# Attention and squared-ReLU FFN in one program: where values are staged, when one square and one pair of transposes run, and which banks hold the last rows

## The chip, the cores and the metric

One core of a Trainium2 chip runs the whole program. The metric is the device time of one execution in microseconds (us); the figure for a kernel is the median of its runs. TensorE (PE) multiplies, ScalarE (ACT) and VectorE (DVE) empty PSUM and do the elementwise work, GpSimd (POOL) casts what has been loaded, and two queues issue transfers: SyncE's (SP) and, for some loads, ScalarE's.

## What is computed

```python
# q, k, v: (8 batches, 8 heads, 576 rows, 64), float32
scores = scale * q @ k.T
mask = (rel >= 0) & (rel < 64)            # causal, window of 64
attn = softmax(where(mask, scores, -1e9))
x = (attn @ v) as (4608 rows, 512)        # heads side by side
h = maximum(x @ w_in, 0)                  # (4608, 2048)
out = (h * h) @ w_out                     # (4608, 512), float32
```

## The kernel before

The 4608 rows are 36 chunks of 128; four chunks make a block of 512 rows, so there are nine blocks, 0 to 8. Two chunks make a pair; pairs 8 and 15 (chunks 16, 17 and 30, 31) are tails, each chunk of which gathers the last 64 rows of two sequences.

**One chunk.** Its k, q and v rows are loaded as float32 into staging tiles (`fetch_kq` L138, `fetch_v` L144, `fetch_tail` L148), cast to fp16 on POOL (`cast_k`, `cast_q`, `cast_v`, through `copy` L248 to L254), turned by DMA transposes on SP (`dma_kT` L345, `dma_qT` L356), multiplied to scores (`S_`, L376), exponentiated on ACT (`expo`, L382), masked on DVE (`keep`, L387), multiplied by v (`V`, L399) and divided by the row sums on DVE (`norm`, L406 and L407). The result x_sb is turned into a part of xT. From block 4 on that is a DMA transpose (`dma_xT`, L426). In the blocks up to 3 it is four TensorE transposes into a PSUM tile (`X`, L418) and a copy out of it on DVE (`copy_xT`).

**One block of the FFN.** The up product has 16 steps (`UP` L474): four matmuls of 512 columns into one of two PSUM buffers (tag `ps_u`, L477), then ReLU on ACT (hrelu, L481), then the square: on ACT for even steps (L483), on DVE for odd ones (L485). DVE reads the PSUM buffer again, so an odd step's buffer is free only after its square. The down product of a block (`out_seven` L534) uses seven half-size products of 8 steps instead of eight. They run in the order A, A again, B, C, D, C again, D again, each product in two halves of 8 matmuls of 256 columns (L556). The first product of A is copied from PSUM to SBUF as p1 by ACT (p, L570), and the second product then goes on adding into the same bank. The other sums u2, u4 and the output rows are made on DVE (L572). The last block uses another bank, E, for the second product, and issues its last product one row half m after the other (`rows_apart` L606, matmuls L608).

**PSUM and staging.** `ps_u`, `ps_o` and `ps_att` have two buffers each; a `ps_att` tile (`att_bank`) is two banks. The staging tag `st` has five single tiles: v of a chunk, q of a tail, and the sums p1, u2 and u4 of the FFN take turns in it. The tag `st2` has six double tiles: k and q of a chunk, or k k and v v of a tail chunk. A tile that is allocated again waits for the readers of what was in it.

**Order.** It is fixed in the program: every engine has a queue in program order. The start (blocks 0 and 1 of the up product, block 0's output) is the hand-written list FIRST. After it, the loop over g from 2 to 9 merges by place in the stage (0 to 1): the 14 steps of `out_seven(g-1)`, the 16 steps UP(g, f), `attention(g+1)` and `loads`. `later(n, fn)` L87 puts an instruction n ticks back; a tick comes after each UP, each half product and each attention step. A stage thus begins with the scores of two chunks, the two halves of A's first product with UP(g, 0) and UP(g, 1) between and behind them, then the copy p.

```python
ev += [(t + 0.02, lambda a=a: sc(a)), ...
       (t + 0.25, lambda a=a: va(a)), (t + 0.251, lambda b=b: va(b)),
       (t + 0.275, lambda a=a: to_xT(a)), (t + 0.276, lambda b=b: to_xT(b))]
```

Here t is 0 or 0.46 for a block's two pairs, and 0.1 more for block 3. v of chunks 22 and up is issued from ACT's queue, everything else from SP's.

Of the kernel before, what the change touches and what calls it, by code (L numbers as in the profile page):

```python
# [41 lines left out]
def kernel(  # L42
# [9 lines left out]
    nc = tc.nc  # L52
# [32 lines left out]
    put_off = []  # L85

    def later(n, fn):  # L87
        put_off.append([n, fn])

    def tick():  # L90
        for e in list(put_off):
# [30 lines left out]
    def fetch_pair(nm, p):  # L122
# [9 lines left out]
        for n in range(2):  # L132
            sts[nm, 2 * p + n] = st[:, :, n, :]

    def two_tiles():
        return stage.tile([P, 2, H, D], FP32, name="kq_st", tag="st2", bufs=6)

# [4 lines left out]
            fetch_rows(sts[nm, i], src, *place(i), eng=eng)  # L142

    def fetch_v(i, eng=nc.sync):  # L144
        sts["v", i] = stage.tile([P, H, D], FP32, name="v_st", tag="st", bufs=5)
        fetch_rows(sts["v", i], v, *place(i), eng=eng)

    def fetch_tail(i):  # L148

        kk, vv = two_tiles(), two_tiles()  # L150
        qv = stage.tile([P, H, D], FP32, name="q_st", tag="st", bufs=5)
        sts["k", i], sts["q", i], sts["v", i] = (kk[:, 0], kk[:, 1]), qv, (vv[:, 0], vv[:, 1])
        b = tail_seq(i)
        for n in range(2):
            fetch_rows(kk[:, n], k, b + n, S - 128)
        for n in range(2):
            fetch_rows(qv[:], q, b + n, S - 64, 64, 64 * n)
        for n in range(2):
            fetch_rows(vv[:, n], v, b + n, S - 128, eng=nc.scalar if i >= 22 else nc.sync)

# [99 lines left out]
        copy(eng, q16s[i][:], sts["q", i])  # L262

    def cast_v(i, eng=nc.gpsimd):
        copy(eng, v_evs[i % NV][:, :, 0:D], sts["v", i][:])

    def shift_v(i, eng=nc.gpsimd):
        v_ev, v_od, v_next = v_evs[i % NV], v_ods[i % NV], v_ods[(i + 1) % NV]
# [205 lines left out]
    def UP(g, f):  # L474
        hps = ps_up.tile([P, 512], FP32, name="hps", tag="ps_u")
        for c in range(DMC):
            nc.tensor.matmul(  # L477
                hps[:], w_in_sb[:, c, f * P:(f + 1) * P], xT_of(g)[:, c, :],
                start=(c == 0), stop=(c == DMC - 1))
        hrelu = hrp.tile([P, 512], FP32, name="hrelu", tag="hrelu")  # L480
        nc.scalar.activation(out=hrelu[:], in_=hps[:], func=AF.Relu)  # L481
        if f in SQ_ACT:
            nc.scalar.activation(out=h2_of(g)[:, f, :], in_=hrelu[:], func=AF.Square)  # L483
        else:
            nc.vector.scalar_tensor_tensor(  # L485
                out=h2_of(g)[:, f, :], in0=hps[:], scalar=0.0, in1=hrelu[:],
                op0=ALU.max, op1=ALU.mult)
        tick()
# [45 lines left out]
    def out_seven(g):  # L534
        h2 = h2s[g]
        TH = 256
        top = (slice(0, TH), slice(0, KH)), (slice(0, TH), slice(KH, FFC))
        bot = (slice(TH, 512), slice(0, KH)), (slice(TH, 512), slice(KH, FFC))
        A = [[h2[:, ks, ts] for ts, ks in row] for row in (top, bot)]
        Sh = [hs_all[:, i] for i in range(2)]  # L540
        Sh += [A[1][0], A[0][1]]
        banks, sums, osb = {}, {}, {}

        def hsum(i, half):
            ks = slice(half * KH // 2, (half + 1) * KH // 2)
            x, y, op = ((A[1][0], A[1][1], ALU.add), (Sh[0], A[0][0], ALU.subtract),
                        (A[0][0], A[1][0], ALU.subtract), (A[0][1], Sh[1], ALU.subtract))[i]
            nc.vector.tensor_tensor(out=Sh[i][:, ks], in0=x[:, ks], in1=y[:, ks], op=op)  # L548

        def product(bank, a, w, half, first):  # L550
            if first and half == 0:
                pool, tag = (ps_up, "ps_u") if bank == "E" else (ps_out, "ps_o")
                banks[bank] = pool.tile([P, 2, NH], FP32, name=f"ops{bank}", tag=tag)
            for kk in range(half * KH // 2, (half + 1) * KH // 2):
                for m in range(2):
                    nc.tensor.matmul(  # L556
                        banks[bank][:, m, :], a[:, kk, m * P:(m + 1) * P], w[:, kk],
                        start=(first and kk == 0 and m == 0), stop=(kk == KH - 1),
                        skip_group_check=True)

        def evac(bank, to, add=None, row=0, col=0, send=False, ms=slice(0, 2)):
            if to == "osb":
                if row not in osb:
                    osb[row] = next_osb()
                dst = osb[row][:, ms, col * NH:(col + 1) * NH]
            else:
                sums[to] = stage.tile([P, 2, NH], FP32, name=to, tag="st", bufs=5)
                dst = sums[to][:]
            if add is None:
                nc.scalar.activation(out=dst, in_=banks[bank][:], func=AF.Copy, scale=OUT_SCALE)  # L570
            else:
                nc.vector.scalar_tensor_tensor(  # L572
                    out=dst, in0=banks[bank][:, ms], scalar=OUT_SCALE, in1=sums[add][:, ms],
                    op0=ALU.mult, op1=ALU.add)
            if send:
                cols = slice(col * NH, (col + 1) * NH) if last else slice(0, DM)
                if is_tail(4 * g + 2 * row):
                    ov = out.rearrange("(b s) d -> b s d", s=S)
                    for n in range(2):
                        b0 = tail_seq(4 * g + 2 * row) + n  # L580
                        nc.sync.dma_start(
                            out=ov[b0:b0 + 3:2, S - 64:S, cols].rearrange("m s d -> s m d"),
                            in_=osb[row][64 * n:64 * n + 64, :, cols])
                else:
                    b, s0 = place(4 * g + 2 * row)
                    r0 = b * S + s0
                    nc.sync.dma_start(
                        out=out[r0:r0 + TH, cols].rearrange("(m p) d -> p m d", p=P)[:, ms],
                        in_=osb[row][:, ms, cols])

        W = [[w_out_sb[:, 0:KH, 0:NH], w_out_sb[:, 0:KH, NH:DM]],
             [w_out_sb[:, KH:FFC, 0:NH], w_out_sb[:, KH:FFC, NH:DM]]]
        last = g == NTB - 1
        plan = [
            ("A", A[0][0], W[0][0], True, (("A", "p1"),)),
            (("E", A[0][1], W[1][0], True, (("E", "osb", "p1", 0, 0, last),)) if last else
             ("A", A[0][1], W[1][0], False, (("A", "osb", None, 0, 0),))),
            ("B", Sh[1], wb[0], True, (("B", "u2", "p1"),)),
            ("C", Sh[0], W[0][1], True, (("C", "u4", "u2"),)),
            ("D", Sh[2], wb[1], True, (("D", "osb", "u4", 1, 1, last),)),  # L600
            ("C", Sh[3], W[1][1], False, (("C", "osb", "u2", 0, 1, True),)),
            ("D", A[1][1], wb[2], False, (("D", "osb", "u2", 1, 0, True),)),
        ]
        before = {0: (0, 1), 2: (2,), 3: (3,)}
        steps = []
        def rows_apart(bank, a, w, m, evs):  # L606
            for kk in range(KH):
                nc.tensor.matmul(banks[bank][:, m, :], a[:, kk, m * P:(m + 1) * P], w[:, kk],  # L608
                                 start=False, stop=(kk == KH - 1), skip_group_check=True)
            for e in evs:  # L610
                evac(*e, ms=slice(m, m + 1))

        for n, (bank, a, w, first, evs) in enumerate(plan):
            if last and n == len(plan) - 1:
                steps += [lambda m=m, args=(bank, a, w): rows_apart(*args, m, evs) for m in range(2)]
                break
            for half in range(2):
                def step(n=n, bank=bank, a=a, w=w, first=first, evs=evs, half=half):
                    for i in before.get(n, ()):
                        hsum(i, half)  # L620
                    product(bank, a, w, half, first)
                    if half == 1:
                        for e in evs:
                            evac(*e)
                    tick()
                steps.append(step)
        return steps
# [24 lines left out]
    def attention(g):  # L652
        c = 4 * g
        ev = []

        def sc(i):
            S_(i)
# [17 lines left out]
        for h in range(2):  # L675
            a, b, t = c + 2 * h, c + 2 * h + 1, 0.46 * h + (0.1 if g == 3 else 0.0)
            ev += [(t + 0.02, lambda a=a: sc(a)), (t + 0.021, lambda b=b: sc(b)),
                   (t + 0.25, lambda a=a: va(a)), (t + 0.251, lambda b=b: va(b)),
                   (t + 0.275, lambda a=a: to_xT(a)), (t + 0.276, lambda b=b: to_xT(b))]
        return ev  # L680

    def load(i):
# [2 lines left out]
            cast_tail(i)  # L685
            return
        fetch_kq(i)
        fetch_v(i, nc.scalar if i >= 22 else nc.sync)
        cast_k(i)
        cast_q(i)  # L690
        cast_v(i)
# [65 lines left out]
```

## Time and profile before

| what | value |
|---|---|
| runs | 305.19 to 311.08 us, median 307.16 (six) |
| the profiled execution's own time | 305.96 us |
| its span, from the first to the last instruction | 304.2 us |
| granted TensorE clock | 1.000 |
| DVE busy | 215.1 us |
| ACT busy | 187.1 us |
| POOL busy | 121.9 us |
| DMA | 57.65 MB, mean 190 GB/s |

The 1.76 us between the time and the span lie before the first and after the last instruction. The profile is one execution; its durations are used below, and the time that is predicted is a median of runs. Times inside the span count from its start. A's first product, which opens a stage, starts at 81.1, 114.7, 143.9, 173.0, 202.7, 233.1 and 261.7 us in the stages with the FFN of two blocks in them, and from 288.0 us only the last block's down product is left. Ends of matmuls are modelled, so PE's waits are best measured from start to start.

### The profile page before, as it was taken

How to read it: one execution, taken by the hardware profiler on the slowest of the kernel's cores; microseconds unless marked ns; L12 is line 12 of the kernel's file. 1: busy time of each engine (PE TensorE's matmuls, PEld its weight loads, DVE VectorE, ACT ScalarE, POOL GpSimd, SP SyncE). 2: the span in 40 equal slices, each digit the busy share in tenths (PEclk: the TensorE clock that was granted, in tenths of full speed). 3: DMA queues.
4: the chain of work that ended last, by engine and by line, in shares of the span. 5: the costliest groups of instructions: out<-in, count | busy, mean ns of one | idle time of the engine just before them, and what ended most of it. 6: DMA issues, size and time to landing. Idle time of an engine off the chain costs nothing.

```text
span 304.2 us, 7566 instructions
## 1 busy us (share of the span) xinstructions
PE 286.8 (94%) x3026; PEld 196.8 (65%) x3026; DVE 215.1 (71%) x397; ACT 187.1 (62%) x303; POOL 121.9 (40%) x176
## 2 busy tenths in 40 slices
PE   1989999999998999999999999999989999999995
PEld 0658788855565566666666656665656666666684
DVE  3668888867876668794978496858575966645392
ACT  3558798795583647665775767576647675656500
POOL 1359854683606326344654456425264500000000
PEclk9999999999999999999999999999999999999999
DMA  7999999993349989999988999999999911300133
GB/s 226 303 394 310 287 270 351 318 245 88 124 108 238 150 217 210 157 209 216 236 195 125 268 210 211 208 247 205 169 179 221 197 37 35 140 0 2 69 105 106
DMA packets 152932, 57.65 MB, mean 190 GB/s; under 512 B 129345, under 2 KB 144705, under 8 KB 152897
## 3 DMA queue, kind: packets, MB, share of 16 engines
q1 hardware_dynamic: 136256, 52.97, 73.3%
q10 hardware_dynamic: 16640, 4.20, 7.1%
q8 instruction: 24, 0.39, 0.6%
q14 instruction: 12, 0.09, 0.1%
HBM read 38.80 MB, written 9.44 MB: 159 GB/s over the span
## 4 chain that ended last, share of the span: by engine, by line
PE 72%; DMA 7%; DVE 6%; POOL 4%; ACT 4%; SPq 4%; issue 3%; POOLq 0%; ACTq 0%
PE hps L477 23%; PE hps L449 9%; PE opsC L556 8%; PE opsD L556 6%; PE opsA L556 5%; PE ops L523 4%; PE opsB L556 4%; PE sc L376 4%; DMA kq_st<-in_k_dram 4%; PE av L399 3%; PE qkT_ps L318 2%; DMA q_st<-in_q_dram 2%; DMA kq_st<-in_q_dram 2%; POOL v_od L252 2%; DVE hs_all L548 1%
## 5 line engine op out<-in xcount | busy, mean ns | idle before, releaser
L477 PE MATMUL hps<-xT,w_in_sb 128*128 128x512 f16 x448 | 112.8, 379 | 2.0 <-DVE h L485 1.2
L481 ACT ACTIVATE hrelu<-hps 128x512 f32<-128x512 f32 x112 | 66.5, 598 | 75.3 <-PE hps L477 66.7
L556 PEld LDWEIGHTS <-h 128*128 128x128 f16 x624 | 60.4, 98 | 22.5 <-issue 2.3
L477 PEld LDWEIGHTS <-w_in_sb 128*128 128x128 f16 x448 | 42.5, 98 | 34.9 <-issue 2.3
L485 DVE SCALAR_TENSOR_TENSOR h<-hps,hrelu 128x512 f16<-128x512 f32 x56 | 38.6, 689 | 37.2 <-ACT hrelu L481 36.9
L252 POOL COPY v_od<-v_ev 64x512 f16<-64x512 f16 x52 | 36.7, 707 | 12.5 <-issue 5.4
L382 ACT ACTIVATE pm<-sc 128x1024 f16<-128x1024 f32 (+1 forms) x40 | 35.6, 936 | 4.1 <-PE sc L376 3.9
L483 ACT ACTIVATE h<-hrelu 128x512 f16<-128x512 f32 x56 | 35.3, 630 | 1.8
L252 POOL CAST k<-kq_st 128x512 f16<-128x512 f32 x18 | 12.7, 704 | 48.5 <-DMA kq_st<-in_k_dram 40.7
L556 PE MATMUL opsA<-w_out_sb,h 128*128 128x256 f16 x240 | 31.0, 273 | 0.6
L556 PE MATMUL opsD<-wb_all,h 128*128 128x256 f16 x240 | 31.0, 273 | 0.0
L556 PEld LDWEIGHTS <-hs_all 128*128 128x128 f16 x256 | 25.1, 98 | 8.9
L449 PE MATMUL hps<-xT,w_in_sb 128*128 128x256 f16 x256 | 30.3, 273 | 0.0
L449 PEld LDWEIGHTS <-w_in_sb 128*128 128x128 f16 x256 | 24.2, 98 | 3.1
L407 DVE TENSOR_TENSOR x_sb<-av,rden 128x512 f16<-128x512 f32 x36 | 24.9, 691 | 1.2
L387 DVE TENSOR_TENSOR pm<-pm,mask_inner 128x1024 f16<-128x1024 f16 x25 | 19.0, 759 | 5.4 <-ACT pm L382 5.3
L252 POOL CAST v_ev<-v_st 128x512 f16<-128x512 f32 x24 | 17.4, 727 | 7.4 <-DMA v_st<-in_v_dram 7.2
L572 DVE SCALAR_TENSOR_TENSOR osb_all<-opsD,u 128x512 f32<-128x512 f32 (+1 forms) x17 | 11.1, 654 | 11.8 <-PE opsD L556 10.5
L376 PEld LDWEIGHTS <-kT 64*128 64x128 f16 x576 | 12.6, 95 | 7.6 <-issue 5.7
L556 PE MATMUL opsC<-w_out_sb,h 128*128 128x256 f16 x128 | 16.4, 273 | 0.0
L556 PE MATMUL opsB<-wb_all,hs_all 128*128 128x256 f16 x128 | 16.4, 273 | 0.0
L556 PE MATMUL opsC<-w_out_sb,hs_all 128*128 128x256 f16 x128 | 16.4, 273 | 0.0
(95 smaller groups left out, 369.5 us busy)
## 6 DMA issues: line engine op xcount, KB each, us to landing
kq_st<-in_k_dram SPq DMA_DIRECT2D x26, 256.0 KB, 3.7
out_dram<-osb_all SPq DMA_DIRECT2D x12, 512.0 KB, 3.9
v_st<-in_v_dram SPq DMA_DIRECT2D x20, 256.0 KB, 4.6
kq_st<-in_q_dram SPq DMA_DIRECT2D x18, 256.0 KB, 4.4
k_st<-in_k_dram SPq DMA_DIRECT2D x7, 512.0 KB, 5.5
q_st<-in_q_dram SPq DMA_DIRECT2D x7, 512.0 KB, 6.3
v_st<-in_v_dram ACTq DMA_DIRECT2D x12, 256.0 KB, 3.9
out_dram<-osb_all SPq DMA_DIRECT2D x11, 256.0 KB, 2.3
```

Of the source, the lines that this page charges most:

```text
L252: eng.tensor_copy(out=out, in_=in_)
L376: nc.tensor.matmul(scv[:, hh, hp, blk, :], kT[r0:r0 + 64, hp, k0:k0 + P], qT, start=i >= 4, stop=True, skip_group_check=i < 4)
L382: nc.scalar.activation(out=pms[i][:, part], in_=scs[i][:, part], func=AF.Exp, scale=1.0 / float(D) ** 0.5)
L387: nc.vector.tensor_tensor(out=pms[i][:, part], in0=pms[i][:, part], in1=mask[:].rearrange("p (o a) r -> p o (a r)", o=1) .to_broadcast([P, ...
L407: nc.vector.tensor_tensor(out=xs[i][:], in0=avs[i][:, :, :, 0:D], in1=rden[:].to_broadcast([P, 2, 4, D]), op=ALU.mult)
L449: nc.tensor.matmul(hps[:, f, :], w_in_sb[:, c, (2 * j + f) * P:(2 * j + f + 1) * P], xT_of(p // 2)[:, c, t0:t0 + 256], start=(c == 0), sto ...
L477: nc.tensor.matmul(hps[:], w_in_sb[:, c, f * P:(f + 1) * P], xT_of(g)[:, c, :], start=(c == 0), stop=(c == DMC - 1))
L481: nc.scalar.activation(out=hrelu[:], in_=hps[:], func=AF.Relu)
L483: nc.scalar.activation(out=h2_of(g)[:, f, :], in_=hrelu[:], func=AF.Square)
L485: nc.vector.scalar_tensor_tensor(out=h2_of(g)[:, f, :], in0=hps[:], scalar=0.0, in1=hrelu[:], op0=ALU.max, op1=ALU.mult)
L523: nc.tensor.matmul(ops_of[ts][:], h2s[0][:, f, ts * P:(ts + 1) * P], w_out_sb[:, f, :], start=(f == 0), stop=(f == FFC - 1))
L556: nc.tensor.matmul(banks[bank][:, m, :], a[:, kk, m * P:(m + 1) * P], w[:, kk], start=(first and kk == 0 and m == 0), stop=(kk == KH - 1), ...
```

## The change

Four things are edited. First, v of the chunks from 22 on (`AHEAD = 22`) and q of the tails no longer take single tiles of tag `st`, but half of a double tile of `st2` that the two chunks of a pair share; `st` keeps v of the early chunks and the FFN's sums. The order of the transfers and their queues stay. Second, the ACT square of step f = 0 of each block goes through `later(2, ...)`; in each of the seven stages that have up products it now stands directly behind the copy p instead of directly ahead of it. Third, in `attention(3)` the step `to_xT` moves from 0.275 to 0.34: its eight transposes, and the two DVE copies that belong to them, go behind one or two UP steps and a half product. Fourth, in the last block bank D is replaced by two, one for each row half m, taken from `ps_att`; its first evacuation becomes two instructions of 256 columns.

```diff
     def later(n, fn):
-        put_off.append([n, fn])
+        if n == 0:
+            fn()
+        else:
+            put_off.append([n, fn])
...
     def fetch_v(i, eng=nc.sync):
-        sts["v", i] = stage.tile([P, H, D], FP32, name="v_st", tag="st", bufs=5)
+        if i < AHEAD:
+            sts["v", i] = stage.tile([P, H, D], FP32, name="v_st", tag="st", bufs=5)
+        elif i % 2 == 0:
+            vv = two_tiles()
+            sts["v", i], sts["v", i + 1] = vv[:, 0], vv[:, 1]
         fetch_rows(sts["v", i], v, *place(i), eng=eng)
...
         kk, vv = two_tiles(), two_tiles()
-        qv = stage.tile([P, H, D], FP32, name="q_st", tag="st", bufs=5)
-        sts["k", i], sts["q", i], sts["v", i] = (kk[:, 0], kk[:, 1]), qv, (vv[:, 0], vv[:, 1])
+        if i % 2 == 0:
+            qq = two_tiles()
+            sts["q", i], sts["q", i + 1] = qq[:, 0], qq[:, 1]
+        sts["k", i], sts["v", i] = (kk[:, 0], kk[:, 1]), (vv[:, 0], vv[:, 1])
...
         if f in SQ_ACT:
-            nc.scalar.activation(out=h2_of(g)[:, f, :], in_=hrelu[:], func=AF.Square)
+            later(2 if f == 0 else 0, lambda: nc.scalar.activation(
+                out=h2_of(g)[:, f, :], in_=hrelu[:], func=AF.Square))
...
+        def rows_of(bank, m):
+            return apart[bank][m][:, 0, :] if bank in apart else banks[bank][:, m, :]
...
-                banks[bank] = pool.tile([P, 2, NH], FP32, name=f"ops{bank}", tag=tag)
+                if last and bank == "D":
+                    apart[bank] = [att_bank(f"opsD{m}")[:, 0:1, 0:NH] for m in range(2)]
+                else:
+                    banks[bank] = pool.tile([P, 2, NH], FP32, name=f"ops{bank}", tag=tag)
...
+            elif bank in apart:
+                for m in range(ms.start, ms.stop):
+                    nc.vector.scalar_tensor_tensor(
+                        out=dst[:, m - ms.start:m - ms.start + 1], in0=apart[bank][m],
+                        scalar=OUT_SCALE, in1=sums[add][:, m:m + 1], op0=ALU.mult, op1=ALU.add)
...
+        dx = 0.34 if g == 3 else 0.275
...
-                   (t + 0.275, lambda a=a: to_xT(a)), (t + 0.276, lambda b=b: to_xT(b))]
+                   (t + dx, lambda a=a: to_xT(a)), (t + dx + 0.001, lambda b=b: to_xT(b))]
```

More of the change, by code (lines that the diff above doesn't have):

```diff
@@ L133, in fetch_pair @@
             sts[nm, 2 * p + n] = st[:, :, n, :]
+    AHEAD = 22
     def two_tiles():
@@ L156, in fetch_tail @@
         for n in range(2):
-            fetch_rows(qv[:], q, b + n, S - 64, 64, 64 * n)
+            fetch_rows(sts["q", i], q, b + n, S - 64, 64, 64 * n)
         for n in range(2):
-            fetch_rows(vv[:, n], v, b + n, S - 128, eng=nc.scalar if i >= 22 else nc.sync)
+            fetch_rows(vv[:, n], v, b + n, S - 128, eng=nc.scalar if i >= AHEAD else nc.sync)
     w_in_sb = const.tile([P, DMC, DFF], FP16, name="w_in_sb")
@@ L264, in cast_v @@
     def cast_v(i, eng=nc.gpsimd):
-        copy(eng, v_evs[i % NV][:, :, 0:D], sts["v", i][:])
+        copy(eng, v_evs[i % NV][:, :, 0:D], sts["v", i])
     def shift_v(i, eng=nc.gpsimd):
@@ L541, in out_seven @@
         Sh += [A[1][0], A[0][1]]
-        banks, sums, osb = {}, {}, {}
+        banks, apart, sums, osb = {}, {}, {}, {}
+        def rows_of(bank, m):
+            return apart[bank][m][:, 0, :] if bank in apart else banks[bank][:, m, :]
         def hsum(i, half):
@@ L556, in product @@
                     nc.tensor.matmul(
-                        banks[bank][:, m, :], a[:, kk, m * P:(m + 1) * P], w[:, kk],
-                        start=(first and kk == 0 and m == 0), stop=(kk == KH - 1),
+                        rows_of(bank, m), a[:, kk, m * P:(m + 1) * P], w[:, kk],
+                        start=(first and kk == 0 and (m == 0 or bank in apart)),
+                        stop=(kk == KH - 1),
                         skip_group_check=True)
@@ L607, in rows_apart @@
             for kk in range(KH):
-                nc.tensor.matmul(banks[bank][:, m, :], a[:, kk, m * P:(m + 1) * P], w[:, kk],
+                nc.tensor.matmul(rows_of(bank, m), a[:, kk, m * P:(m + 1) * P], w[:, kk],
                                  start=False, stop=(kk == KH - 1), skip_group_check=True)
@@ L687, in load @@
         fetch_kq(i)
-        fetch_v(i, nc.scalar if i >= 22 else nc.sync)
+        fetch_v(i, nc.scalar if i >= AHEAD else nc.sync)
         cast_k(i)
```

## The prediction

> **What bounds the kernel now.** I read the page first: shares of the engines, and the two rows of slices for PE's load and its granted clock.
>
> ```profile
> span 304.2 us, 7566 instructions
> PE 286.8 (94%) x3026; PEld 196.8 (65%) x3026; DVE 215.1 (71%) x397; ACT 187.1 (62%) x303; POOL 121.9 (40%) x176
> PE   1989999999998999999999999999989999999995
> PEclk9999999999999999999999999999999999999999
> ```
>
> TensorE is busy in all but the first and the last slices, at full clock. No other engine reaches 75%, so what can be won is PE's waiting. But PE's modelled ends hide short waits, so I went to the timeline of PE and compared starts. Here is the opening of the stage at 114.7 us, PE first, then ACT in the same window:
>
> ```profile
> 115.62 1.03 PE L477 MATMUL hps<-xT,w_in_sb 128*128 128x512 f16 x4
> 116.49 1.04 PE L556 MATMUL opsA<-w_out_sb,h 128*128 128x256 f16 x8
> 117.36 1.03 PE L477 MATMUL hps<-xT,w_in_sb 128*128 128x512 f16 x4
> 118.48 1.03 PE L556 MATMUL opsA<-w_out_sb,h 128*128 128x256 f16 x8
> ```
>
> ```profile
> 116.69 0.60 ACT L481 ACTIVATE hrelu<-hps 128x512 f32<-128x512 f32 x1
> 117.31 0.63 ACT L483 ACTIVATE h<-hrelu 128x512 f16<-128x512 f32 x1
> 117.85 0.58 ACT L570 ACTIVATE p<-opsA 128x512 f32<-128x512 f32 x1
> ```
>
> Four up matmuls take 0.87 us from start to start (115.62 to 116.49), but 1.12 us in front of the second product of A (117.36 to 118.48): PE waits 0.25 us there. The second product adds into A's bank, which p has to read first, and p ends at 118.43. It starts 0.54 us behind the square's start; A's first half product had ended, as modelled, at 117.53. So the square delays it.
>
> Then block 3's transposes and the last rows:
>
> ```profile
> 92.58 0.40 PE L418 MATMUL xt_ps<-ident,x_sb 128*128 128x128 f16 x4 [0.80 <-DVE x_sb L407]
> 93.42 0.40 PE L418 MATMUL xt_ps<-ident,x_sb 128*128 128x128 f16 x4 [0.44 <-DVE x_sb L407]
> 93.65 1.03 PE L477 MATMUL hps<-xT,w_in_sb 128*128 128x512 f16 x4
> ```
>
> ```profile
> 298.52 1.04 PE L608 MATMUL opsD<-wb_all,h 128*128 128x256 f16 x8
> 300.07 1.03 PE L608 MATMUL opsD<-wb_all,h 128*128 128x256 f16 x8 [0.52 <-DVE osb_all L572]
> ```
>
> The bracket is PE's idle time and what ended it. In the chain that ended last the V matmuls end at 91.57, then DVE's two normalisations are on the path until 93.37.
>
> **The change, part by part.**
>
> Transposes later. At the first place PE goes from 91.57 to 93.65, 2.08 us, with eight transposes between, which cost 2 x 0.23 (93.42 to 93.65): 1.6 us of it is waiting. Behind the change an up step, half of B and another up step come first, 0.87 + 0.87 + 0.87 = 2.6 us; x_sb needs 1.8 us (91.57 to 93.37), so nothing is left to wait for. The up step that now follows V needs a free buffer: step 3's square was over at 90.77. At the second place the four transposes of the second chunk start at 109.50 instead of 108.70 + 0.23 = 108.93: 0.57 us. Half of D and an up step come between, so the transposes stand 2.6 us behind V instead of 0.9, again more than 1.8. The number of transposes is unchanged, and the step issues no transfer. Their two DVE copies (0.42 us each) go behind one square, a sum and u2 at the first place, behind one square at the second. Who waits for them: the next pair's scores, for the PSUM tile (99.82 and 114.17 before, over 3 us behind the new place), and the next stage's up product. Queued behind them on DVE are a 0.7 us sum and a square that are due over 1 us later. I cost them at nothing; without that cover it is at most 2 x 0.42 per place. Gain 2.2 us.
>
> First square behind p. p needs A's half product (117.53) and hrelu out of the way (117.29): it starts at 117.57, ends at 118.15, and the next product could start at 117.36 + 0.87 = 118.23. The 0.25 us go, barely. All of the six stages from 114.7 on show the same 1.12 us in front of that product (118.48, 147.62, 176.75, 206.44, 237.02, 265.48); the stage at 81 us has no wait, since its scores stand in that place. What is late next: hrelu of step 1 (118.42) comes 0.25 later, and DVE squares it only at 120.68. PE comes 0.25 earlier to step 3, which needs that square's buffer. Ends of the square and starts of step 3: 121.36 and 121.82; 150.62 and 150.96; 240.16 and 240.36; 266.74 and 268.08. That leaves 0.25, 0.25, 0.20 and 0.25. At 176.75 the gain is lost: PE stands at 180.65 with 0.49 us of idle behind DVE, whose queue does not move. At 206.44 it is lost too: PE waits 0.29 us at 212.84 behind an hrelu that was held until 209.83 by ACT's issue of a v load. Sum 0.95 us, and 1.5 us if all six counted.
>
> Here the Trainium skill weighs in (SBUF, section "SBUF: two separate sides"): a DVE instruction with two SBUF inputs and a GpSimd instruction take the shared pair of ports exclusively, so one blocks the other. The trace shows hs_all (two SBUF inputs) at 0.68 us alone and 1.09 to 1.13 us beside POOL's casts, as at 174.70 and 175.83: a delay shorter than the whole cast (0.61 or more). If the casts fell elsewhere, 0.68 for each of the four hs_all before 180.65 would take about 1.6 us off that queue, and the stage would keep its 0.25 and its 0.49. With contention as traced it keeps nothing. I take the traced one: the change moves no cast on POOL.
>
> Double tiles. Nothing is computed more and no transfer moves on its queue. Removed: p's wait for the reader of an old v or q tile. In all six stages p starts 0.53 to 0.54 us behind the square, so that wait never bound: gain 0. Added: an even chunk's v load on ACT's queue, and the tails', wait for the cast of the double tile six places back; ReLUs are queued behind it, and PE behind those. The tightest is chunk 31: issued at 197.73, while the casts of chunk 29's k and q ended at 190.38, 7.3 us earlier. On SP the reuse is covered by transposes that already wait for later casts. Cost 0; with the cover gone, see the last rival. A gain isn't excluded where an execution has late casts.
>
> Last rows. The second D group starts at 300.07, but 298.52 + 0.87 = 299.39 is its pace: 0.68 us. Its evacuation (301.14, 0.42 us) and the last store follow directly, and the queue is free: the store before it is issued from 300.05 on. The first evacuation becomes 2 x 0.42 instead of 0.69 on DVE at 296.98; its bank is used again at 298.52, so the extra 0.15 is hidden. Gain 0.68 us.
>
> Sum: 2.2 + 0.95 + 0.68 = 3.8 us. Profiled execution: 305.96 (304.2 of span and 1.76 around it) - 3.8 = 302.1. It was 1.2 us below the median of the six runs; 307.16 - 3.8 = 303.3 is my number.
>
> **The rivals.**
>
> More (0.14). All six p waits go, 1.5 us instead of 0.95, and what puts the median 1.2 us above the profiled execution is p held by late casts, which the double tiles end: 305.96 - 4.4 = 301.6. For it: the runs differ by more than a microsecond, so something that this profile doesn't show varies. Against it: in the profile no p waits for a cast.
>
> Absorbed (0.14). The DMA engines are at 1.00 to 1.08 of their time from 114 to 237 us. If loads are paced by themselves, ACT's holds at 209.83 and at 223.51 (2.46 us) stay where they are, and all that PE won before them is lost: 0.20 + 0.25 + 0.68 = 1.1 remains, 306.0. Against it: SP waits for DVE in every stage (36.9 us for output rows, 14.5 of it outside the longest wait, and 8.6 us in ten waits ahead of the transposes of x_sb), so it follows the compute engines.
>
> Without the square's part (within the likeliest case): if the accumulating product waits for something other than p, 0.95 goes, 304.3.
>
> Slower (0.06). The new waits of the v loads bind. Place: ACT's queue, at the eight loads that open a double tile (chunks 22, 24, 26, 28, 30, 31, 32, 34). Price: ACT's idle of 2.46 us at 223.51 cost PE 0.79 us idle, 0.95 from start to start. Eight of those are 7.6 us, less the 3.8: 310.9. It decides once the cast of the tile six back ends later than ACT comes to the load, that is once the 7.3 us of slack at the tightest are used up; at four holds it is even. Against it: POOL waits for loads (40.7 us for k alone), it is not behind.
>
> **How the numbers follow.** Likeliest, 0.66: 303.3, by itself 302.2 to 304.5. A measurement of this kernel can tell about 0.5%, so faster means below 305.6 and slower above 308.7. Faster is the likeliest and "more", 0.66 + 0.14, and a small part of "absorbed", 0.81; same the rest of "absorbed", 0.13; slower 0.06. The range 301.0 to 306.0 leaves out the slower case and half of the absorbed one.
>
> **What would show it.** Right: the transposes of block 3 without idle time; 0.87 to 0.9 us from the up step to A's second product in each stage; the last D group 0.87 us behind the first. Wrong: 1.12 us still there although p stands before the square; ACT idle for over 2 us in front of more v loads than 209 and 223 us; a longer wait of PE for h (L485) behind V, which would be the gain given back.

## The result and the profile after

The changed kernel takes 305.9 us (median of 34 runs, 303.9 to 309.7) beside 307.2 us of the kernel before (71 runs): a ratio of 0.9955, 95% interval 0.9940 to 0.9971, so 1.4 us less (0.9 to 1.8) where 3.8 were forecast. Measured twice more beside the experiments, it stood at 0.9918 (0.9890 to 0.9947) and at 0.9959 (0.9924 to 0.9994). The profiled execution took 306.02 us with 304.2 of span, as long as the one of before (305.96 and 304.2).

From the page, the span, the shares of the engines and PE's slices:

```profile
span 304.2 us, 7559 instructions
PE 285.9 (94%) x3026; PEld 197.0 (65%) x3026; DVE 216.2 (71%) x398; ACT 186.4 (61%) x303; POOL 119.9 (39%) x176
PE   1989999999999999979899999999989999999996
```

The dip that stood at 91 us (the 8 in slice 13 of before) is gone. New are a 7 and an 8 near 133 and 145 us. PE's busy time is nearly the same (286.8 us before) and so is the span, so what was saved in one place was waited for in another.

The timeline of PE shows the three places of the change (start, duration, line, operation; idle time in brackets):

```profile
93.48 1.03 PE L489 MATMUL hps<-xT,w_in_sb 128*128 128x512 f16 x4
94.35 0.61 PE L430 MATMUL xt_ps<-ident,x_sb 128*128 128x128 f16 x8
...
113.72 1.03 PE L489 MATMUL hps<-xT,w_in_sb 128*128 128x512 f16 x4
114.58 1.04 PE L577 MATMUL opsA<-w_out_sb,h 128*128 128x256 f16 x8
115.45 1.03 PE L489 MATMUL hps<-xT,w_in_sb 128*128 128x512 f16 x4
116.31 1.04 PE L577 MATMUL opsA<-w_out_sb,h 128*128 128x256 f16 x8
...
299.26 1.91 PE L635 MATMUL opsD<-wb_all,h 128*128 128x256 f16 x16
```

Block 3's eight transposes follow the up step without idle time. A's second product starts 0.86 us behind its up step (115.45 to 116.31), no longer 1.12. Both groups of D run as one piece. Every wait that the prediction wanted to remove is removed. New waits stand elsewhere; these are the first two of them, in the timeline of ACT and its queue, of SP's queue, and of PE:

```profile
129.92 0.63 ACT L496 ACTIVATE h<-hrelu 128x512 f16<-128x512 f32 x1
133.32 0.43 ACTq L122 DMA_DIRECT2D kq_st<-in_v_dram  x1
133.80 1.09 ACT L493 ACTIVATE hrelu<-hps 128x512 f32<-128x512 f32 x2 [3.25 <-PE av L411]
```

```profile
125.26 3.94 SPq L438 DMA_TRANSPOSE xT<-x_sb  x2
129.25 0.57 SPq L122 DMA_DIRECT2D kq_st<-in_k_dram  x1
129.88 0.57 SPq L122 DMA_DIRECT2D kq_st<-in_q_dram  x1
...
139.36 3.27 SPq L438 DMA_TRANSPOSE xT<-x_sb  x2
```

```profile
134.94 1.02 PE L489 MATMUL hps<-xT,w_in_sb 128*128 128x512 f16 x4 [1.58 <-ACT hrelu L493]
...
145.73 1.02 PE L489 MATMUL hps<-xT,w_in_sb 128*128 128x512 f16 x4 [1.12 <-ACT pm L394]
```

ACT has nothing left at 130.55 and stands until 133.25. In the program its next instruction, the issue of chunk 22's v, waits on a semaphore that it shares with the q load of chunk 21. SP issued that load at 129.88, and in the chain of waits it lands 3.35 us later, at 133.23. Two ReLUs stand behind the issue, and PE behind them. The kernel before had the same order. These are its lines, SP's and then ACT's:

```profile
128.96 0.57 SPq L119 DMA_DIRECT2D kq_st<-in_q_dram  x1
...
138.39 2.52 SPq L426 DMA_TRANSPOSE xT<-x_sb  x2
```

```profile
132.01 0.63 ACT L483 ACTIVATE h<-hrelu 128x512 f16<-128x512 f32 x1
132.69 0.44 ACTq L119 DMA_DIRECT2D v_st<-in_v_dram  x1
```

There the q load landed at 132.59 and ACT had work until 132.64, so the wait had a cover of 0.05 us and did not show. PE is 1.9 us earlier now; SP is 0.9 us later.

The second wait, 1.12 us ahead of 145.73, is put down to ACT, but the trace has PE's sequencer held until 145.68 at a semaphore of the transposed x: the second of the two transposes from 139.36 on landed at 145.64. In the kernel before it landed at 143.40, and PE came to it at 144.76, so that there 1.36 us were to spare. The two waits, 2.7 us together, are what this execution lost: PE was 1.9 us ahead of the kernel before at the start of the second stage (112.83 beside 114.74), 0.3 at the third, and 0.75 us behind at the fourth (173.76 beside 173.01).

### The profile page after: what moved, and what is told of

The parts are those of the page before. It is cut to its first block, busy times and chain, and to the rows that moved or that the text cites. A ratio compares the mean times of both kernels' runs of the same rounds, so it can differ in the third digit from the quotient of the medians.

```text
span 304.2 us, 7559 instructions
## 1 busy us (share of the span) xinstructions
PE 285.9 (94%) x3026; PEld 197.0 (65%) x3026; DVE 216.2 (71%) x398; ACT 186.4 (61%) x303; POOL 119.9 (39%) x176
## 4 chain that ended last, share of the span: by engine, by line
PE 76%; DMA 7%; DVE 5%; ACT 4%; SPq 3%; issue 2%; POOL 2%; ACTq 0%; DVEq 0%; POOLq 0%
PE hps L489 26%; PE hps L461 9%; PE opsC L577 8%; PE opsD L577 6%; PE opsA L577 6%; PE ops L537 4%; PE opsB L577 4%; PE sc L388 4%; PE av L411 3%; DMA kq_st<-in_k_dram 3%; PE qkT_ps L330 2%; DMA q_st<-in_q_dram 2%; ACT pm L394 2%; DVE hs_all L565 1%; DMA kT<-k 1%
## 5 line engine op out<-in xcount | busy, mean ns | idle before, releaser
L264 POOL COPY v_od<-v_ev 64x512 f16<-64x512 f16 x52 | 36.9, 711 | 12.9 <-issue 5.4
L399 DVE TENSOR_TENSOR pm<-pm,mask_inner 128x1024 f16<-128x1024 f16 x25 | 20.9, 835 | 5.2 <-ACT pm L394 5.1
L264 POOL CAST q<-kq_st 128x512 f16<-128x512 f32 x22 | 15.6, 708 | 9.8 <-DMA kq_st<-in_q_dram 9.7
L388 PE MATMUL sc<-qT,kT 64*128 64x64 f16 x576 | 15.9, 203 | 0.4 <-DVE qT L264 0.4
```

What stands on the lines that cost most here:

```text
L264: eng.tensor_copy(out=out, in_=in_)
L388: nc.tensor.matmul(scv[:, hh, hp, blk, :], kT[r0:r0 + 64, hp, k0:k0 + P], qT, start=i >= 4, stop=True, skip_group_check=i < 4)
L399: nc.vector.tensor_tensor(out=pms[i][:, part], in0=pms[i][:, part], in1=mask[:].rearrange("p (o a) r -> p o (a r)", o=1) .to_broadcast([P, ...
```

## The experiments

Two theories at first. **The loads' queue paces**: between 114 and 233 us SP's queue, and what waits for its transfers, sets the end, so that what PE wins before or inside this stretch is lost there to new waits. **The double tiles give it back**: they were costed at nothing and aren't free. What separates them is the time by stages, so I cut every trace at the starts of A's first products, as in the section on the profile before. The columns are one stage (81 to 114 us in the kernel before), the four stages from 114 to 233 us together, the last of these four (203 to 233), and all behind it; us, one execution each.

| kernel | stage at 81 | four stages | last of them | rest |
|---|---|---|---|---|
| before | 33.65 | 118.4 | 30.4 | 71.0 |
| x_only | 31.48 | 121.3 | 32.2 | 71.3 |
| square_only | 33.64 | 121.1 | 32.5 | 70.4 |
| rows_only | 33.64 | 118.7 | 30.9 | 70.3 |
| tiles_only | 33.64 | 119.0 | 30.2 | 71.4 |
| the change, three executions | 31.71, 31.71, 31.58 | 121.7, 121.4, 122.0 | 31.1, 33.8, 33.6 | 69.7, 69.7, 70.1 |
| without double tiles, three | 31.58, 31.58, 31.70 | 118.4, 119.5, 122.4 | 30.7, 31.6, 32.4 | 70.4, 69.9, 70.5 |
| v_tiles | 31.89 | 119.2 | 31.6 | 69.7 |
| q_tiles | 31.84 | 120.2 | 30.9 | 69.7 |
| v_on_sp | 31.57 | 126.2 | 37.8 | 73.6 |
| no_tiles_v_pool | 31.51 | 121.5 | 34.6 | 70.2 |
| after_v_pool | 31.90 | 117.3 | 30.3 | 70.7 |
| no_tiles_st_pool | 31.58 | 119.6 | 29.8 | 70.1 |
| before_nostore | 33.64 | 117.4 | 29.5 | 70.9 |
| after_nostore | 31.58 | 117.9 | 29.8 | 69.7 |
| no_tiles_nostore | 31.83 | 116.9 | 29.3 | 70.4 |

### Each part alone

**x_only**, against the kernel before:

```diff
+        dx = 0.34 if g == 3 else 0.275
-                   (t + 0.275, lambda a=a: to_xT(a)), (t + 0.276, lambda b=b: to_xT(b))]
+                   (t + dx, lambda a=a: to_xT(a)), (t + dx + 0.001, lambda b=b: to_xT(b))]
```

> Of the four parts only one is made: block 3's transposes on TensorE later. The step of the prediction says -2.2 us, ratio 0.993. Theory 'the queue of the loads paces 114 to 237 us' (whatever TensorE wins before 114 us is waited away before 237 us, behind ScalarE's issues of v loads and in front of the transposed x) says 0 to -0.5 us, ratio 0.998 to 1.000; the three waits of block 3's transposes are gone in the trace, and TensorE's waits between 114 and 237 us are some 2 us longer than in the kernel before.

Measured 0.9949 (0.9924 to 0.9973), -1.6 us (-2.3 to -0.8). Its stage at 81 us is 2.2 us shorter, as forecast, and the same wait as in the whole change stands at 133.86 us, 1.36 us long, in a kernel without the double tiles. The interval holds the forecast and not the "0 to -0.5" of the strict form of the first theory.

**square_only**, against the kernel before:

```diff
-            nc.scalar.activation(out=h2_of(g)[:, f, :], in_=hrelu[:], func=AF.Square)
+            later(2 if f == 0 else 0, lambda: nc.scalar.activation(
+                out=h2_of(g)[:, f, :], in_=hrelu[:], func=AF.Square))
```

> Only the first square behind p. The step of the prediction says -0.95 us (0.25 at four stages kept, at two lost), ratio 0.997. Theory 'the loads' queue paces 114 to 237 us' keeps only the stages behind 226 us, 0.20 + 0.25 = 0.45 us, ratio 0.9985.

0.9964 (0.9937 to 0.9991), -1.1 us (-1.9 to -0.3): both sizes lie in it. The trace shows where the gain is sure: the stages at 233 and 262 us go from 28.62 to 28.24 and from 26.29 to 26.04. In the stages at 115, 145 and 175 us the 0.25 are won and a wait for DVE's square of step 1 stands behind V, here in the first:

```profile
122.99 1.24 PE L487 MATMUL hps<-xT,w_in_sb 128*128 128x512 f16 x5 [0.53 <-DVE h L497]
```

**rows_only**, against the kernel before:

```diff
-                banks[bank] = pool.tile([P, 2, NH], FP32, name=f"ops{bank}", tag=tag)
+                if last and bank == "D":
+                    apart[bank] = [att_bank(f"opsD{m}")[:, 0:1, 0:NH] for m in range(2)]
...
```

> Only the last rows in two banks. It lies behind every load, so both theories say the same, -0.68 us, ratio 0.998: the second group of D 0.87 us behind the first, not 1.55.

0.9967 (0.9943 to 0.9991), -1.0 us (-1.8 to -0.3); in the trace the end behind 288 us is 15.43 long instead of 16.11, so the 0.68 of the forecast.

**tiles_only**, against the kernel before (the tails' q likewise):

```diff
+        elif i % 2 == 0:
+            vv = two_tiles()
+            sts["v", i], sts["v", i + 1] = vv[:, 0], vv[:, 1]
...
```

> Only the double tiles for v and for the tails' q. The step of the prediction says 0. Theory 'the loads' queue paces 114 to 237 us' says 0 too. Theory 'the double tiles give it back' (six buffers that held six chunks of k and q hold four chunks with their v, so SyncE's loads of k and q and ScalarE's of v wait for later casts) says +2.2 to +2.5 us, ratio 1.007 to 1.008: what the whole change lacks.

1.0026 (1.0003 to 1.0048), +0.8 us (+0.1 to +1.5): not nothing, and not the 2.2 of the second theory. The four add up to -2.9, by their intervals -4.4 to -1.4. So each of the three gains, taken alone, holds its forecast in its interval; the 0 of the double tiles lies outside of its own.

### The three without the double tiles, and all v loads on SP

**no_tiles**, against the changed kernel (the tails' q likewise):

```diff
-        if i < AHEAD:
+        if True:
             sts["v", i] = stage.tile([P, H, D], FP32, name="v_st", tag="st", bufs=5)
```

> The whole change except the double tiles: transposes later, square behind p, last rows in two banks, with v and the tails' q in single tiles as in the kernel before. Alone, the three measured -1.5, -1.1 and -1.0 us, the double tiles +0.8. Theory 'the double tiles give it back' says the three add up, -3.0 to -3.6 us, ratio 0.988 to 0.990. Theory 'the loads' queue paces 114 to 237 us' says no more than the whole change, -1.4 us, ratio 0.995, with ScalarE's hold at the first v load it issues (chunk 22) and TensorE's wait for that hrelu near 133 us of 1.3 us or more.

0.9885 (0.9844 to 0.9926), -3.5 us, six runs. It looked like a clear win for the second theory, and the stretch is as short in its trace as before the change (118.4). It did not last, as the repetitions below show.

**v_on_sp**, against the changed kernel (the tails' v likewise):

```diff
-        fetch_v(i, nc.scalar if i >= AHEAD else nc.sync)
+        fetch_v(i, nc.sync)
```

> The changed kernel with all v loads issued by SyncE, none by ScalarE. If ScalarE's holds at these issues are what takes the gain back, they are gone (no idle over 2 us on ScalarE between 114 and 237 us, TensorE's wait of 1.58 us at 133 and 1.18 us at 225 us gone) and the kernel is 1 to 2.5 us faster than the change, ratio to the kernel before 0.987 to 0.992. If SyncE's queue is the pace itself, the same wait comes back in front of the transposed x and the ratio stays at 0.995 or rises, since SyncE has 14 more transfers to issue.

1.019 (1.0144 to 1.0235), 5.9 us slower than the kernel before. ACT's holds are gone and PE waits for SP's transposes instead, in the stage of the tails 30 and 31 above all:

```profile
205.86 1.89 PE L489 MATMUL hps<-xT,w_in_sb 128*128 128x512 f16 x4 [4.25 <-DMA xT<-x_sb]
222.75 0.41 PE L388 MATMUL sc<-qT,kT 64*128 64x64 f16 x16 [1.41 <-DMA qT<-q]
```

SP's queue has sixteen transfers more (the tails' v are two loads each, so not 14), eleven of them in the four stages, and these are 4 to 5 us longer. Not all of that is waiting: behind the wait of 4.25 us the granted clock was 0.50 from 206 to 210 us and 0.81 from 210 to 215, which by these shares is an estimated 3 us of PE's work. The rest says that this queue has little room there. The rows of its transfers fill 110.7 of 121.7 us (91%) in the changed kernel, 108.0 of 118.4 (91%) in the one before, and 117.8 of 126.2 here.

### Without stores

Both runs leave out the stores of blocks 1 to 7.

**after_nostore**, against the changed kernel, and **before_nostore**, the same in the kernel before:

```diff
-            if send:
+            if send and last:
```

> The changed kernel without the stores of the output rows of blocks 1 to 7 (only those of blocks 0 and 8 are written). SyncE then waits for no output row and has less to move. To be read against the next run, the kernel before without the same stores. Theory 'the loads' queue paces 114 to 237 us' says that the pair differs by the forecast 3 to 3.8 us. Theory 'the double tiles give it back' says that it still differs by about 1.4 us.

> The kernel before without the stores of the output rows of blocks 1 to 7. If SyncE's queue paces 114 to 237 us in the kernel before too, it is 1 us or more faster than with them; if TensorE does, it is the same within 0.5 us.

0.9823 (0.9790 to 0.9856) and 0.9908 (0.9876 to 0.9940), 302.7 and 305.1 us. The kernel before is 2.8 us faster without these stores, although PE computes the same: its end was set by the transfers too, not by PE alone. SP's rows fill 85 to 87% of the four stages now, and these are nearly as long in the changed kernel as in the one before (117.9 and 117.4): next to nothing of what PE wins ahead of them is given back. The pair differs by 2.4 us, more than with stores (1.4) and less than the 3.8 forecast; its interval, about 1.2 to 4.0 us, holds both, so here the stages say more than the medians.

The missing stores leave SP's queue shorter and the DMA engines less to move, and this pair can't tell the two apart. In the four stages the engines' share of busy time was 0.96 to 1.14 before and 0.80 to 1.02 without the stores.

### The double tiles once more

**no_tiles_2** and **after_2** are no_tiles and the changed kernel again, **v_tiles** and **q_tiles** have half of the double tiles each.

> The change without the double tiles once more, beside the next three on one chip. If the double tiles take back what is missing, it stays at 0.987 to 0.991 of the kernel before and is 1.5 to 2.5 us faster than the whole change; if the first measurement of it was a lucky one, it is at 0.993 to 0.996.

> The whole change once more. Both theories: 0.994 to 0.997 of the kernel before. Its trace is a second execution: where TensorE waits between 114 and 237 us in both executions of it and not in those without the double tiles is where they cost; waits that stand at other places in the two are variation.

On one chip: 0.9896 (0.9851 to 0.9941) without and 0.9918 (0.9890 to 0.9947) with the double tiles. The second trace of the change has no wait at 133 us. It waits at another place, again for a transfer of SP:

```profile
202.36 1.04 PE L489 MATMUL hps<-xT,w_in_sb 128*128 128x512 f16 x4 [1.47 <-DMA xT<-x_sb]
```

So the waits move from execution to execution inside the stretch, while the sum of the four stages stays (121.7 and 121.4). The second of these two transposes had been issued at 196.30 and landed at 202.31, 6.0 us later; in the third execution of the change (after_3) it was issued at 198.67 and landed at 205.73, and PE waited 2.05 us for it. In the kernel before the same transpose took 4.8 us to land. Set against the start of PE's stage, the issue was 2.1 and 1.6 us later than before, and the landing took 1.2 and 2.3 us longer on top.

> The change with the tails' q in single tiles again, v from chunk 22 on in double tiles. If ScalarE's and SyncE's waits for v and its double tiles cost (14 loads), it is as slow as the whole change, 0.994 to 0.997; if the tails' q does, it is as fast as without double tiles, 0.987 to 0.991.

> The change with v in single tiles again, only the tails' q (chunks 16, 17, 30, 31) in double tiles, where it takes a buffer of the k and q loads. The other way round from the run ahead: 0.987 to 0.991 if v's double tiles cost, 0.994 to 0.997 if the tails' q does.

Half of the double tiles each: 0.9913 (0.9880 to 0.9947) and 0.9926 (0.9901 to 0.9950). Neither stands apart, and the four stages took 119.2 and 120.2 us; this says nothing on which half costs.

> The change without the double tiles, beside the whole change on one chip, to settle the size of what the double tiles cost. Theory 'they take back 1 to 2 us': 303.4 to 304 us here and 304.6 to 306 us in the next run. Theory 'they cost nothing, the loads' queue does it': the two within 0.5 us of each other.

> The whole change beside the run ahead: 1 to 2 us slower than it if the double tiles cost, within 0.5 us if they don't. In the stretch from the second to the seventh stage, 113 to 232 us, TensorE's time is 120.5 us or more in the first case, and at most 119.5 us, as without double tiles, in the second.

Again on one chip: 0.9949 (0.9923 to 0.9975) without and 0.9959 (0.9924 to 0.9994) with them. The four stages took 122.4 us without double tiles. So the loss does not need them: this execution and x_only (121.3) have it without. The second theory as the whole cause falls with that. A cost of about 1 us is not ruled out: it was 0.8 (0.1 to 1.5) alone, the three measurements without double tiles spread over -3.5, -3.2 and -1.6 us, and two of their three executions kept most of the gain (118.4 and 119.5).

### Whose queue it is

**no_tiles_v_pool** and **after_v_pool**, against the changed kernel without and with the double tiles (the tails' v likewise):

```diff
-        fetch_v(i, nc.scalar if i >= AHEAD else nc.sync)
+        fetch_v(i, nc.gpsimd if i >= AHEAD else nc.sync)
```

> The change without the double tiles, with the v loads of chunk 22 on issued by GpSimd instead of ScalarE; nothing is left out. ScalarE's holds in front of them (2.3 us at 208 and 222 us, TensorE's waits of 0.8 to 1.6 us behind) then can't be. If the holds are how the pace of the loads reaches TensorE, the stretch from the fourth to the seventh stage shortens by 1.5 to 2 us and the kernel is at 0.982 to 0.985 of the kernel before. If SyncE's queue is, TensorE waits as long in front of the transposed x, and it stays at 0.988 to 0.990.

> The whole change, double tiles too, with the v loads of chunk 22 on issued by GpSimd. If the double tiles cost by what ScalarE waits for at these issues, this one is equal to the run ahead within 0.5 us. If it is slower by 0.8 us or more, the cost of the double tiles has another way, the order of the transfers themselves.

0.9952 (0.9930 to 0.9975) and 0.9925 (0.9892 to 0.9958). No v load holds ACT any more, and that the time is better than with the holds is not shown. In the first, PE waits for the transposed q instead:

```profile
214.02 0.41 PE L386 MATMUL sc<-qT,kT 64*128 64x64 f16 x16 [0.23 <-DMA qT<-q]
217.27 0.61 PE L386 MATMUL sc<-qT,kT 64*128 64x64 f16 x16 [2.84 <-DMA qT<-q]
```

Its four stages took 121.5 us, of which the granted clock of 0.61 from 217.3 to 221.3, behind that wait, is an estimated 1.6. In the second no such wait is longer than 0.52 us, and the four stages took 117.3. So ACT's holds are one way in which late transfers reach PE, and not the only one. Both expectations missed: without double tiles this kernel is not faster but perhaps slower than with them. In the program, GpSimd's loads into single tiles wait for the sums that share the tag, and those into double tiles don't.

**no_tiles_nostore** has the edits of no_tiles and of after_nostore.

> The change without the double tiles and without the stores of the output rows of blocks 1 to 7. With the double tiles this was 302.7 us, the kernel before in the same way 305.1. If the double tiles cost only where SyncE's queue is full, it is at 302.7 too (0.982 to 0.983); if they cost by themselves, at 301.2 to 301.8 (0.977 to 0.979), the forecast 3.8 below the kernel before without the stores.

0.9836 (0.9807 to 0.9866), 302.4 us, as with double tiles (302.7, on another chip): with fewer transfers they cost nothing that can be seen.

**no_tiles_st_pool**, without the double tiles, both stores in `out_seven`:

```diff
-                    nc.sync.dma_start(
+                    (nc.sync if last else nc.gpsimd).dma_start(
```

> The change without the double tiles, with the stores of blocks 1 to 7 issued by GpSimd instead of SyncE; nothing is left out. SyncE then waits for no output row and has 16 transfers less to issue, while the bytes moved stay. If SyncE's order paces the stretch, it is at 0.980 to 0.984 of the kernel before; if the bytes do, it stays at 0.988 to 0.990; GpSimd's casts that stand behind its waits for the rows could make it slower, above 0.992.

0.9865 (0.9824 to 0.9905), 303.2 us, the lowest median of a kernel that leaves nothing out. Its interval overlaps that of two of the three runs without double tiles (0.9885, 0.9896, 0.9949), so that it is better is not shown. Its four stages took 119.6 us: this execution does not show that a relief of SP's order alone gives what the missing stores gave (116.9).

## Why the prediction was wrong

**The failed step is the sum**: it carried what PE wins at 92, 109, 118 and 148 us to the end, and set "absorbed" aside with "it follows the compute engines". The trace of before says otherwise. Of the 36.9 us that SP waited for output rows, 0.4 stand ahead of 257 us; the rest stands behind the last load, where nothing is left to pace. The 8.6 us in ten waits are put down to squares and sums of h, not to x_sb: from 114 to 237 us SP came to 14 of its 16 transposes of x_sb 0.4 to 5.8 us after x_sb was ready, and it waited 0.4 and 0.2 us for the other two. So in this stretch SP hardly followed DVE at all.

SP's own time agrees. From its first transpose in the stage at 81 us (82.40 before) to the q load behind the last output rows ahead of 233 us (233.24) it took 150.8 us before, and 151.5, 150.7 and 152.0 in the three executions of the change, although PE's stage at 81 us was 2 us shorter in these; square_only, rows_only and tiles_only took 152.3, 152.1 and 151.4, x_only 151.6. PE's gain did not move SP in these. Without the double tiles it took 148.5, 148.2 and 152.6, so a shorter time is possible; why it came in two of these three is open. Before, ACT could have come 0.05 us earlier to the v load at 133 us, and PE 1.36 us earlier to the transposed x at 145 us, without waiting; the forecast for the stage ahead was 2.2.

This is the chain of waits of the kernel before, start, duration and what it was, between 197 and 225 us:

```profile
196.98 0.89 PE opsC L556 x8
...
199.35 1.47 SPq L581
...
200.88 4.30 DMA kq_st<-in_k_dram
...
205.23 1.03 POOL k L289
...
211.35 1.38 SPq L351
...
214.10 3.23 DMA kq_st<-in_k_dram
```

And of the changed one:

```profile
200.33 1.06 SPq L608
...
201.44 4.69 DMA kq_st<-in_k_dram
...
212.88 1.22 SPq L363
...
215.46 3.20 DMA kq_st<-in_k_dram
...
221.07 3.87 DMA kT<-k
...
226.06 1.02 PE hps L489 x4
```

In both the end does not hang on PE for a time from 198 us on, but on a store, a load behind it in SP's queue, its cast, three transposes, the next load and its transposes; in the changed kernel it comes back to PE at 226.06. That was to be read before. The chain alone would not have decided it, since it enters this part from PE's product C; and the changed kernel's first execution had lost its lead by 173 us, at the two waits shown further up.

Point by point:

- **Transposes later, -2.2.** Right at its place: the stage goes from 33.64 us to between 31.5 and 31.9. Alone -1.6 (-2.3 to -0.8).
- **Square behind p, -0.95.** Right in mechanism, 0.86 to 0.91 instead of 1.12 in each stage. Of the two late stages, forecast 0.20 and 0.25, come 0.4 and 0.25. Of the two early ones, square_only gives the 0.25 back where the prediction said it would show if it was wrong: PE's wait for h behind V, 0.53 and 0.57 us. In the three executions of the change this wait is about 0.2 us at most. The slack of 0.46 us (121.36 to 121.82) was that of one execution: tiles_only, where no square moves, has a wait of 0.47 us there too.
- **Double tiles, 0.** Alone +0.8 (0.1 to 1.5), with the rest between 1.0 and -0.4 us in the two pairs on one chip (304.6 to 303.6 us and 306.6 to 307.0). No wait that they add was found to bind: in the trace of the change ACT's long holds end with the landing of a transfer of SP on the semaphore that the v load uses too, not with a cast. Alone it is a second term that the sum had too small; what costs is open.
- **Last rows, -0.68.** Right, 16.11 to 15.43.
- **What was not in the sum**: the four stages from 114 to 233 us, 118.4 to 121.1 us (mean 119.3) in the four executions with stores and with the transposes where they were, and 121.4 to 122.0 in the three of the change. That is 2.4 us given back; -2.0 at 81 us, +2.4, and -1.2 behind 233 make -0.8, and the medians -1.4 to -2.5. The size is loose, since one execution differs from the next by 2 us or more in this stretch. Over all nine executions with the transposes moved, and the stores and v loads on the queues of before, the four stages average 120.7 us, so 1.4 given back. The sign rests on the two waits of the change's trace that end with a transfer's landing, on SP's time, which the change left at 151 to 152 us, and on the pair without stores, where the four stages differ by 0.5 us.

The rival "absorbed" gave 306.0 by this mechanism, with ACT's holds at 209 and 223 us as the place. The holds are there (2.5 us ahead of 210.38, 2.4 ahead of 224.50), and one more at 133 us. They end in the same way as that one: a transpose of k lands at 210.20, a q load at 224.40, each on the semaphore of the v load. Taking them away moved waits to qT and xT in v_on_sp and no_tiles_v_pool. The rival deserved the larger chance.

What stays open: whether the order in SP's queue or the DMA engines behind it are what is full (no run changes one alone, except no_tiles_st_pool, whose time lies between the two answers); why SP's transposes take 1.5 us in one execution and 2.6 in the next at the same place (xT at 125 us: 1.52 in the first trace without double tiles and 2.63 in that of the change, with x_sb ready 2.9 and 3.8 us before); and whether the double tiles have a part in it.

## What to carry to other kernels

Before summing up what an engine will win, list the transfers that it or its neighbours wait for behind that place, and set each one's landing against its use: a win larger than this slack (here 0.05 and 1.36 us) is at risk unless the transfers come earlier too, and what is won behind the last of them is sure. Whether a queue follows an engine is read from its waits inside the stretch in question, not from their sum over the kernel. How full its rows are does not tell it alone: SP's rows fill 87% of the four stages in square_only and in tiles_only (121.1 and 119.0 us) as in the changed kernel without stores (117.9). And where executions differ by as much as the change is worth, one trace cannot say where the gain went: cut several by stages and compare the sums.

## What was not expected of the hardware

- A transpose from SBUF to SBUF of 128 KB holds SP's queue for 1.19 us at least, a load of 256 KB for 0.46 at least and 0.57 in the median. The 51 transposes from 114 to 237 us take 73.7 of SP's 113 us in the kernel before (74.6 of 112 in the changed one). The Trainium skill (Advanced Engine Details and Errata, section "X-Bar Transpose (TRN2)") calls such transfers as fast as regular ones. From issue to landing they take about as long (medians, in the changed kernel from 114 to 150 us, of 3.7 and 3.8 us for kT and qT, 3.8 and 4.6 for the loads of k and q), though a load moves twice the bytes; in the issuing queue they take twice as long, and the measurement decides.
- The same transposes at the same place in the queue hold it for different times, as xT at 125 us above; four stages together differ by 4 us between executions (118.4 and 122.4 without double tiles), while the stage at 81 us differs by 0.1 in the same three (31.58 to 31.70).
- Two long waits of PE were followed by a lower clock, which makes them cost more than their length: the granted clock was 0.50 for 4 us behind the wait of 4.25 us in v_on_sp and 0.61 for 4 us behind that of 2.84 in no_tiles_v_pool, but 1.00 behind the 2.05 us of after_3.
